# The last six first-layer weight units of an attention and maxout kernel: an integer add and a subtraction in place of identity products on TensorE, and new ranks in the planner

## The chip, the cores and the metric

The kernel runs on one core of one Trainium2 chip. The metric is the device time of one execution, in microseconds (us). The engines are TensorE (PE in the rows; its weight loads are PEld), VectorE (DVE), ScalarE (ACT), GpSimd (POOL) and SyncE (SP), which issues most DMAs.

## The reference

Attention over 8 batches, 8 heads, 576 positions and 64 values a head, with a mask that lets a position see its own block of 64 and all blocks before it; its output, 4608 tokens of 512 values, goes through three products of which the largest is kept, and through a last product:

```python
scores = np.matmul(q, k.transpose(0, 1, 3, 2)) / np.sqrt(D)
scores = np.where(mask, scores, -1000000000.0)     # mask: block_i >= block_j, blocks of 64
attn = np.exp(scores - np.max(scores, axis=-1, keepdims=True))
attn = attn / (np.sum(attn, axis=-1, keepdims=True) + 1e-09)
attn_out = np.matmul(attn, v)
x = attn_out.transpose(0, 2, 1, 3).reshape(B * S, H * D)
h = np.maximum(np.maximum(x @ w1, x @ w2), x @ w3)  # 512 -> 768
out = h @ w_out                                     # 768 -> 512
```

The weights reach the chip as 64-bit numbers, and each is read as a low and a high 32-bit word; q, k and v have 32 bits.

## The kernel before

**Pairs.** Attention goes by pairs of heads: 8 batches of 4 pairs, numbered 0 to 31. For each pair TensorE makes the scores (L924, L931), VectorE the row maxima (L448), ScalarE the exponentials (L615, L950), ScalarE and GpSimd the normalised values (L464, L466). From batch 1 on VectorE turns them (L635, L639) into the tile pz, SyncE moves pz to pt by DMA (L645), and TensorE multiplies pt by v (L1005); batch 0 is turned on TensorE (L569, L976). VectorE also turns q and k (L908).

**Chunks.** The second half of the program goes by nine chunks of 512 tokens. Chunks 0 to 7 are the first 512 positions of batches 0 to 7; chunk 8 gathers the remaining 64 positions of all batches. A chunk needs the x of its four pairs, each split into a rounded part xh (ScalarE) and a rest xl (a subtraction, L261, on GpSimd or VectorE). Then 18 products, one for each weight unit of the first layer (216 matmuls, L1129), with the largest of three kept in the tile m (L1142); then the projection through w_out (72 matmuls, L1163), whose left side is m split into hh and hl. There is one m: the products of the next chunk beyond its first one wait for the projection.

**Weight units.** A weight unit is a tile of 128 by 512 weights. Units 0 to 17 belong to the first layer (w1, w2, w3 in turn for each of six column blocks), units 18 to 23 to w_out. A unit is loaded by SyncE (L308) and rebuilt from its words into a rounded part h and a rest l. For units 0 to 17 the steps are: `size` (ScalarE, L331), `clamp` (L336), `shift` (L343), `sign` (L349), `power` (L360), `rest` (L370), all five on VectorE; `high` (ScalarE, a cast at L256); `summed`, three matmuls with an identity or its negative (L376 to L378) that add up the value, minus h, plus the rest in PSUM; and `lower_summed`, a cast from PSUM (ScalarE, L256). Units 18 to 23 have `size`, `tail` (L326, ScalarE or VectorE), `clamp`, `shift`, `sign`, `whole` (an int32 add, L357), `high`, and `lower`, the subtraction of h from the value (L261, GpSimd or VectorE). Temporaries lie in the tiles wo0 to wo3 for units 0 to 17, with wo4 or wo5 as a spare until the sum is made; the w_out units use wo4, wo5 and the two osb tiles, and are themselves kept in wo0 to wo5. The negative identity lies in one of the osb tiles.

**The order.** No engine's order is written out. Each step is a job with a rank, a modelled duration for each engine that may do it, the jobs that it follows and the buffers that it takes. `in_order` plays the jobs on the modelled engines: whenever an engine is idle, it takes the ready job of lowest rank. The order that comes out is what each engine then does. Ranks come from a few numbers: pair p of batch 0 has rank p x FIRST_PAIR, later pairs follow in steps of PAIR, unit u has DELAY + PACE x u (its load 8 less), and a chunk spreads its products over the ranks from its start to the next chunk's start, where a start is the rank behind its batch's last pair, plus END.

Of the kernel before, what the change touches and what calls it, by code (L numbers as in the profile page):

```python
# [143 lines left out]
def pe(*cols, least=128):  # L144
    return sum(max(n, least) / 2.4 + 13.5 for n in cols)


def dve(n, fast=False):
    return 68.0 + n / (1.92 if fast else 0.96)


def act(n, psum=True):
    return (52.0 if psum else 88.0) + n / 1.2


def pool(n):
    return 150.0 + 2.15 * n
# [3 lines left out]
def kernel(  # L161
# [19 lines left out]
    NF = DF // P  # L181
    NT = 4
    HALF = (256, 320)
    SCALE = 0.125
    DELAY = 28.0
    PACE = 3.5

    PAIR = 24
    FIRST_PAIR = 14
    TURN = 12  # L190

    SECOND = 9
    NEAR = 4
    END = 40
    N = 512

    slots = dict(
# [48 lines left out]
    def job(cost, rank, call, *args, after=(), take=(), give=(), lasts=0.0, moved=0.0, ports=False):  # L246
        j = Job(cost, rank, lambda eng: call(eng, *args), after, take, give, lasts, moved, ports)
        jobs.append(j)
        return j
# [14 lines left out]
    class Unit:  # L264


        def __init__(self, u, src, dst, n, prior, *early, first=None):
            self.src, self.dst, self.n, self.u = src, dst, n, u
            self.last = n == DO
            rank = DELAY + PACE * u  # L270


            self.tag = f"wo{dst}" if self.last else f"w{u}"
            self.temps = (f"wo{u % 4}",) if not self.last else (f"wo{4 + dst % 2}",) if dst < 4 else ("osb", "osb")
            j = self.issued = job(
                {"SP": SEND},
                rank - 8,
                self.load,
                after=(prior and prior.issued, first, *(e.sized for e in early if e)),
                take=(self.tag,) if self.last else (),  # L280
            )
            j = job({}, 0, lambda eng: None, after=(j,), lasts=MOVE, moved=1600.0)
            j = self.sized = job({"ACT": act(512, False) + 65.0}, rank, self.size, after=(j,), take=self.temps)
            if not self.last:
                spare = f"wo{4 + u % 2}"
                for step, fast in (
                    (self.clamp, True),
                    (self.shift, True),
                    (self.sign, False),
                    (self.power, True),  # L290
                    (self.rest, False),
                ):
                    c = dve(512, fast) + (5.0 if fast else 5.0)
                    j = job({"DVE": c}, rank, step, after=(j,), take=(spare,) if step == self.rest else (), lasts=c + GAP, ports=True)
                j = job({"ACT": act(512, False)}, rank, self.high, after=(j,))
                j = job({"PE": 6 * pe(512)}, rank, self.summed, after=(j,), take=("pm",), give=(*self.temps, spare))
                self.done = job({"ACT": act(512)}, rank, self.lower_summed, after=(j,), give=("pm",))
                return
            k = job({"ACT": act(512, False) + 65.0, "DVE": dve(512) + 5.0}, rank, self.tail, after=(j,))
            for step, fast in ((self.clamp, True), (self.shift, True), (self.sign, False), (self.whole, False)):  # L300
                c = dve(512, fast) + (5.0 if fast else 5.0)
                j = job({"DVE": c}, rank, step, after=(j, k) if step == self.whole else (j,), lasts=c + GAP, ports=True)
            h = job({"ACT": act(512, False)}, rank, self.high, after=(j,))
            self.done = job({"POOL": pool(512), "DVE": dve(512) + 5.0}, rank, self.lower, after=(h,), give=self.temps, ports=True)
# [90 lines left out]
    units, begun = {}, []  # L395

    def weights():
        u, prior, early = 0, None, []
        for f in range(NF):
            for i, w in enumerate((w1, w2, w3)):  # L400
                prior = units[i, f] = Unit(
                    u, w[:, f * P : (f + 1) * P].rearrange("(c p) f -> p c f", p=P), (i, f), P, prior, early[u - NEAR] if u >= NEAR else None, first=begun[min(u + 1, NP - 1)]
                )
                early.append(prior)
                u += 1
        for f in range(NF):
            prior = units["out", f] = Unit(
                u,
                w_out[f * P : (f + 1) * P, :].rearrange("(c p) f -> p c f", p=P),
                f,  # L410
                DO,
                prior,
                early[2 * NF + f],
                early[u - 2],
            )
            early.append(prior)
            u += 1
# [41 lines left out]
    def norm_cost(n):  # L459
        return {"POOL": 250.0 + 1.5 * n, "ACT": 190.0 + n / 1.2}  # L460
# [7 lines left out]
    class Head:  # L468
# [5 lines left out]
        def plan(self, t0):  # L474

            pair, part, self.exps, self.inv = self.pair, self.pair.part, {}, {}
            for n, ts in enumerate(part.groups):
                apart, r = None, t0 + (SECOND if part.beside and ts == part.later else n)
                for t in ts:
                    m = P * (t + 1)  # L480
                    d = job(
                        {"DVE": dve(m) + 20.0},
                        r + 1,
                        self.top,
                        t,
                        after=(pair.scored[ts], apart, pair.began),
                        take=("stat",) if pair.began is None else (),
                    )
                    pair.began = pair.began or d
                    if t != ts[-1]:  # L490
                        apart = job({}, 0, lambda eng: None, after=(d,), lasts=GAP)
                    self.exps[t] = job({"ACT": act(m) + 200.0}, r + 2, self.exp, t, after=(d,), take=(f"p{t}",))
                join([self.exps[t] for t in ts], BANK)

        def turns(self, t0, after):
# [4 lines left out]
            for t in part.tiles:  # L500
                r = t0 + 8 + t / 2 + (SECOND if part.beside and t in part.later else 0)
                self.scales[t] = job(norm_cost(P * (t + 1)), r, self.scale, t, after=(self.inv[t],))
# [146 lines left out]
    class Pair:  # L649
# [11 lines left out]
        def plan(self, first, before):  # L661
# [42 lines left out]
            if part.beside:  # L704
                self.later = job(
                    {"PE": cost[part.later] + 200.0 + before.cost},
                    first + SECOND,
                    self.both,
# [3 lines left out]
                self.scored[part.later] = self.later  # L712
                before.finish(self.later, first + SECOND)
            else:
# [8 lines left out]
            for j, h in enumerate(self.heads):  # L723
                h.plan(first + 4 * j)
            for r, ts in ((first + 7, [t for g in part.first for t in g]), (first + SECOND + 5, part.later)):
                r = r if ts != part.later or part.beside else first + 8
# [455 lines left out]
    made = []  # L1182

    def plan(b, part, gap):
        nonlocal rank
        pairs = [Pair(b, hp, part, len(made) + hp) for hp in range(NP)]
        for p in pairs:
            p.plan(rank, made[-1] if made else None)
            made.append(p)
            rank += gap  # L1190
        return pairs

    rank = 0
    pairs, starts = [], []
    for b in range(B):
        pairs.append(plan(b, PLAIN if b == 0 else EARLY if b == 1 else WHOLE, PAIR if b else FIRST_PAIR))
        starts.append(rank + END)
    made[-1].alone(rank + SECOND)
    starts += [starts[-1] + NP * PAIR, starts[-1] + 2 * NP * PAIR]
    weights()  # L1200
    last = units[2, NF - 1].done
    job({"SP": 1.0}, -100, lambda eng: None, take=("osb",))
    join((last,), ("osb",))

# [36 lines left out]
```

## Time and profile before

| what | value |
|---|---|
| median of 3 runs | 894.97 us (894.92 to 895.81) |
| time of the profiled execution | 897.37 us |
| its span, first to last instruction | 895.6 us |
| TensorE busy | 873.8 us, 98% |
| VectorE busy | 561.5 us, 63% |
| ScalarE busy | 443.3 us, 50% |
| GpSimd busy | 148.7 us, 17% |
| granted TensorE clock | 1.000 over the whole span |

The shares are means over stages that differ. The records of matmuls overlap, since they are pipelined, so 98% does not say that every matmul follows the one before at full pace; the start of one to the start of the next does.

### The profile page before, as it was taken

What the parts mean: (1) busy time and instruction counts of PE and PEld (TensorE: products, weight loads), DVE (VectorE), ACT (ScalarE), POOL (GpSimd) and SP (SyncE); (2) the same over time, 40 slices, a digit from 0 to 9 for tenths busy, and PEclk for the clock granted to TensorE, in tenths of its full rate; (3) what the DMA queues carried; (4) which work ended last, traced back from release to release, by engine and by line L of the source; (5) the groups of instructions that cost most, each with busy time, mean ns of one, the idle gap of its engine ahead of it and who ended that gap; (6) DMA issues with size and microseconds to landing.
All of it is one profiled execution on the core that took longest, in us unless ns stands there. A gap on an engine that the chain in (4) does not pass through costs nothing.

```text
span 895.6 us, 13551 instructions
## 1 busy us (share of the span) xinstructions
PE 873.8 (98%) x4436; PEld 647.3 (72%) x4436; DVE 561.5 (63%) x1545; ACT 443.3 (50%) x1225; POOL 148.7 (17%) x179
## 2 busy tenths in 40 slices
PE   6889999999999999999999999999999999999997
PEld 4666667767777767777767777777777778888886
DVE  4799999968767576837773876477656732122121
ACT  5677577666546354645555454555455523013012
POOL 1001214321113012301221121212130201001000
PEclk9999999999999999999999999999999999999999
DMA  6565546676665266526654565555555430000002
GB/s 151 166 175 135 118 103 192 131 162 140 136 138 125 66 134 138 120 89 132 126 119 117 119 127 118 127 125 115 114 137 112 112 74 36 12 0 36 12 1 47
DMA packets 228549, 97.10 MB, mean 108 GB/s; under 512 B 185216, under 2 KB 223104, under 8 KB 228480
## 3 DMA queue, kind: packets, MB, share of 16 engines
q1 hardware_dynamic: 214208, 93.89, 45.3%
q10 hardware_dynamic: 14272, 2.36, 1.5%
q8 instruction: 35, 0.57, 0.3%
q14 instruction: 34, 0.28, 0.1%
HBM read 40.89 MB, written 9.44 MB: 56 GB/s over the span
## 4 chain that ended last, share of the span: by engine, by line
PE 86%; DVE 7%; ACT 2%; DMA 1%; SPq 1%; issue 1%; DVEq 0%; ACTq 0%
PE pm L1129 47%; PE pm L1163 16%; PE sb L1005 9%; PE sb L924 8%; PE sb L931 3%; DVE sb L448 2%; PE sb L569 2%; PE pm L376 1%; DVE pz L635 1%; SPq L645 1%; DMA pt<-pz 1%; ACT p L615 1%; DVE kq L908 0%; DVE m L1142 0%; ACT p L950 0%
## 5 line engine op out<-in xcount | busy, mean ns | idle before, releaser
L1129 PE MATMUL pm<-xh,w 128*128 128x512 f32 x1296 | 434.0, 403 | 0.0
L1129 PEld LDWEIGHTS pm<-xh,w 128*128 128x128 f32 x1296 | 243.3, 188 | 64.9 <-issue 13.2
L1129 PE MATMUL pm<-xl,w 128*128 128x512 f32 x648 | 253.2, 391 | 0.8 <-POOL xl L261 0.8
L615 ACT ACTIVATE p<-sb,nm 128x512 f32<-128x512 f32 (+3 forms) x256 | 133.6, 527 | 89.7 <-DVE nm L448 88.3
L448 DVE CUSTOM_DVE_ANT_0 sb<-sb,mask 128x512 f32<-128x512 f32 (+3 forms) x288 | 143.3, 528 | 53.8 <-PE sb L931 36.4
L635 DVE STREAM_TRANSPOSE pz<-p 128x512 f32<-128x512 f32 (+1 forms) x280 | 138.1, 528 | 38.8 <-ACT p L464 24.4
L466 POOL TENSOR_TENSOR p<-p,rs 128x128 f32<-128x128 f32 (+3 forms) x107 | 73.4, 704 | 464.7 <-DVE rs L759 407.9
L1142 DVE TENSOR_TENSOR m<-pm,m 128x512 f32<-128x512 f32 x108 | 73.2, 678 | 110.7 <-PE pm L1129 108.7
L1129 PEld LDWEIGHTS pm<-xl,w 128*128 128x128 f32 x648 | 121.9, 188 | 28.1 <-issue 4.5
L1163 PE MATMUL pm<-wo,hh 128*128 128x512 f32 x432 | 133.4, 390 | 0.4 <-ACT hh L256 0.4
L1163 PEld LDWEIGHTS pm<-wo,hh 128*128 128x128 f32 x432 | 80.9, 188 | 17.9 <-ACT hh L256 1.0
L1005 PE MATMUL sb<-pt,vn 128*64 128x320 f32 (+2 forms) x840 | 91.7, 361 | 1.4 <-DMA pt<-pz 1.3
L924 PE MATMUL sb<-kq 64*128 64x128 f32 (+3 forms) x512 | 88.5, 463 | 2.9 <-DVE rs L759 1.4
L1005 PEld LDWEIGHTS sb<-pt,vn 128*64 128x64 f32 x840 | 56.1, 137 | 40.3 <-issue 10.6
L1163 PE MATMUL pm<-wo,hl 128*128 128x512 f32 x216 | 84.2, 390 | 0.6 <-DVE hl L261 0.6
L924 PEld LDWEIGHTS sb<-kq 64*128 64x128 f32 x512 | 45.3, 189 | 44.7 <-issue 20.8
L256 ACT COPY m<-pm 128x512 f32<-128x512 f32 x54 | 31.5, 583 | 87.7 <-PE pm L1129 87.6
L464 ACT ACTIVATE p<-p,rs 128x384 f32<-128x384 f32 (+3 forms) x117 | 64.3, 591 | 20.7 <-DVE rs L759 20.6
L261 DVE TENSOR_TENSOR hl<-m,hh 128x384 fp32r<-128x384 f32 x55 | 34.0, 627 | 52.5 <-ACT hh L256 51.8
L256 ACT CAST hh<-m 128x384 fp32r<-128x384 f32 x72 | 35.1, 512 | 56.3 <-PE pm L1163 40.9
L256 ACT COPY x<-sb 128x256 f32<-128x256 f32 x59 | 22.0, 374 | 59.6 <-PE sb L1005 59.4
L615 ACT ACTIVATION_READ_ACCUMULATOR p<-sb,nm 128x1 f32 x256 | 50.9, 199 | 0.0
(91 smaller groups left out, 742.1 us busy)
## 6 DMA issues: line engine op xcount, KB each, us to landing
pt<-pz SPq DMA_DIRECT2D x224, 200.0 KB, 3.9
w<-in_moe_w_dram SPq DMA_DIRECT2D x18, 512.0 KB, 5.3
vn<-in_v_dram SPq DMA_DIRECT2D x64, 128.0 KB, 2.3
out_dram<-osb SPq DMA_DIRECT2D x32, 256.0 KB, 2.0
nat<-in_k_dram SPq DMA_DIRECT2D x112, 72.0 KB, 2.3
nat<-in_q_dram SPq DMA_DIRECT2D x96, 72.0 KB, 2.4
wo<-in_moe_w_out_dram SPq DMA_DIRECT2D x6, 512.0 KB, 4.1
nat<-in_q_dram ACTq DMA_DIRECT2D x16, 72.0 KB, 3.4
```

The lines of the kernel that those rows point to most:

```text
L256: nc.scalar.copy(dst, src)
L261: {"DVE": nc.vector, "POOL": nc.gpsimd}[eng].tensor_tensor(out=dst, in0=a, in1=b, op=ALU.subtract)
L448: nc.vector.tensor_tensor_reduce(out=ps, in0=ps, in1=hidden, scale=-SCALE, scalar=first, op0=ALU.add, op1=ALU.min, accum_out=out_)
L464: nc.scalar.mul(p, p, r)
L466: nc.gpsimd.tensor_tensor(out=p, in0=p, in1=r.broadcast_to([P, p.shape[1]]), op=ALU.mult)
L615: nc.scalar.activation(dst, src, AF.Exp, bias=nm[:, c : c + 1], scale=-1.0, accum_out=sm[:, c : c + 1])
L635: nc.vector.transpose(dst, p[:, 0 : n * P])
L924: nc.tensor.matmul(ps, self.q[h.own, P * t : P * (t + 1)], self.k[h.own, 0:w], start=True, stop=True)
L1005: nc.tensor.matmul(o[h.own].rearrange("p (i u) -> p i u", u=n)[:, :, c0 : c0 + z - a], self.vn[:, kt, h.j, :], h.pt[:, :, a:z], start=(m = ...
L1129: nc.tensor.matmul(self.ps, w[i, f][:, c, :], xx, start=(c == 0 and s == 0), stop=(c == NC - 1 and s == 2))
L1142: nc.vector.tensor_tensor(out=m, in0=ps, in1=m, op=ALU.max)
L1163: nc.tensor.matmul(self.po, h, w[f], start=(f == 0 and s == 0), stop=(f == NF - 1 and s == 2))
```

## The change

Units 12 to 17 go the way of the w_out units: `tail` and `whole` in place of `power` and `rest`, and `lower` in place of `summed` and `lower_summed`. They no longer take a PSUM bank or the spare tile. The negative identity's osb tile is given back after unit 11 and not after unit 17. The constants of the planner's ranks are changed, and units, the first twelve pairs and the chunks get corrections of their own.

```diff
-    DELAY = 28.0
+    DELAY = 28.1
     PACE = 3.5
-    PAIR = 24
-    FIRST_PAIR = 14
+    PAIR = 24.0
+    FIRST_PAIR = 12.7
     TURN = 12
     SECOND = 9
+    SUMMED = 12
+    UNITS = (0, 0, 0, 0, -1, 0, 0, 4, 9, 9, 1, 9, 9, 9, 9, 8, 8, 8, 8, 8, 8, 8, 8, 7)
+    PAIRS = (0, 0, 0, 0, 0, 0, 0, 0, -2, -2, -4, -2)
+    STARTS = (-1, -1, -2, -1, -1, -1, -1, -1, 3, -1, 2)
     NEAR = 4
-    END = 40
+    END = 33.6
...
-            rank = DELAY + PACE * u
+            rank = DELAY + PACE * u + UNITS[u]
...
-            if not self.last:
+            if u < SUMMED:
                 spare = f"wo{4 + u % 2}"
...
-            p.plan(rank, made[-1] if made else None)
+            p.plan(rank + (PAIRS[len(made)] if len(made) < len(PAIRS) else 0), made[-1] if made else None)
...
     starts += [starts[-1] + NP * PAIR, starts[-1] + 2 * NP * PAIR]
+    starts = [a + d for a, d in zip(starts, STARTS)]
     weights()
-    last = units[2, NF - 1].done
+    last = [x for x in units.values() if x.u < SUMMED][-1].done
```

The steps that units 12 to 17 now take are those of the w_out units:

```python
def tail(self, eng):    # b = low_word * 2**-29, as int32; ACT or DVE
def whole(self, eng):   # a = a + b, int32; DVE
def lower(self, eng):   # l = a - h; POOL or DVE
```

## Rows read from the trace of the kernel before

**Rows 1.** The page: busy time, share of the span and instructions of each engine.
```profile
PE 873.8 (98%) x4436; PEld 647.3 (72%) x4436; DVE 561.5 (63%) x1545; ACT 443.3 (50%) x1225; POOL 148.7 (17%) x179
```

**Rows 2.** Busy time by stretch: PE, PEld, DVE, ACT, POOL, then PE's clock and DMA.
```profile
45.00:95.00 50.00, 45.36 (x284) 30.81 (x281) 48.97 (x147) 38.65 (x110) 9.67 (x10) 1.00 0.58 146
95.00:130.00 35.00, 34.71 (x153) 22.32 (x153) 34.21 (x86) 21.39 (x53) 4.84 (x5) 1.00 0.44 100
130.00:178.80 48.80, 48.80 (x252) 35.34 (x249) 47.38 (x125) 33.98 (x89) 18.38 (x18) 1.00 0.70 169
...
203.90:762.00 558.10, 556.72 (x2847) 410.24 (x2846) 359.47 (x1009) 285.79 (x815) 99.81 (x121) 1.00 0.52 115
```

**Rows 3.** Chain that ended last, 86 to 128 us: start, length, what.
```profile
93.25 1.38 DVE wo L360
...
108.55 0.86 PE pm L376 x2
109.41 0.23 PE pm L377
109.64 0.24 PE pm L378
...
119.74 0.59 ACT w L256
...
127.55 0.86 PE pm L376 x2
```

**Rows 4.** The same chain where TensorE is full: 204 products in a row.
```profile
762.51 46.24 PE pm L1129 x204
```

**Rows 5.** Unit steps, 95 to 130 us: count, duration ns min/median/max, first and last start.
```profile
L370 DVE SCALAR_TENSOR_TENSOR wo<-w,wo x8: 679/684/691, 94.7 to 126.1; 128x512 fp32r<-128x512 uint32 x8
...
L360 DVE TENSOR_SCALAR wo<-wo x7: 389/423/427, 97.7 to 125.0; 128x512 int32<-128x512 int32 x7
```

**Rows 6.** The w_out units' own steps: the tail, the integer add, the subtraction.
```profile
L326 ACT ACTIVATE wo<-wo x4: 654/670/692, 131.9 to 145.2; 128x512 int32<-128x512 uint32 x4
...
L357 DVE CUSTOM_DVE_ANT_0 osb<-osb x2: 643/666/689, 158.1 to 164.7; 128x1024 uint16<-128x1024 uint16 x2
...
L261 POOL TENSOR_TENSOR wo<-osb,wo 128x512 fp32r<-128x512 f32 x2 | 2.6, 1296 | 8.4 <-ACT p L615 5.8 <-ACT wo L256 2.6
```

**Rows 7.** The cast from PSUM, 85 to 130 us, on ScalarE: count, busy us, mean ns.
```profile
L256 ACT CAST w<-pm 128x512 fp32r<-128x512 f32 x9 | 5.2, 578 | 2.4 <-PE pm L378 2.4
```

**Rows 8.** VectorE and GpSimd around the w_out subtractions: start, duration, instruction.
```profile
143.39 1.49 DVE L343 TENSOR_SCALAR wo<-wo 128x512 int32<-128x512 int32 x1
...
146.94 0.41 DVE L343 TENSOR_SCALAR wo<-wo 128x512 int32<-128x512 int32 x1
...
148.41 1.44 DVE L357 CUSTOM_DVE_ANT_0 wo<-wo 128x1024 uint16<-128x1024 uint16 x1
...
143.30 1.29 POOL L261 TENSOR_TENSOR wo<-wo,wo 128x512 fp32r<-128x512 f32 x1 [1.33 <-ACT wo L256]
```

**Rows 9.** L1129 alone by stretch: PE busy (matmuls), PEld busy (loads).
```profile
95.00:150.80 55.80, 31.86 (x133) 24.30 (x132) 1.00 0.55 138
```

**Rows 10.** From chunk 0 to chunk 1: GpSimd and TensorE by time.
```profile
166.63 1.30 POOL L261 TENSOR_TENSOR wo<-osb,wo 128x512 fp32r<-128x512 f32 x1 [5.79 <-ACT p L615]
...
192.24 1.30 POOL L261 TENSOR_TENSOR xl<-x,xh 128x512 fp32r<-128x512 f32 x1 [5.31 <-ACT xh L256]
...
182.78 0.62 PE L1163 MATMUL pm<-wo,hh 128*128 128x512 f32 x2
...
186.30 2.93 PE L1005 MATMUL sb<-pt,vn 128*64 128x320 f32 x28
...
202.14 0.50 PE L1129 MATMUL pm<-xh,w 128*128 128x512 f32 x1
```

**Rows 11.** Loads of units, SyncE's queue: count, issue ns, first and last issue.
```profile
L308 SPq DMA_DIRECT2D w<-in_moe_w_dram x18: 367/510/977, 9.5 to 93.0; - x18
L308 SPq DMA_DIRECT2D wo<-in_moe_w_out_dram x6: 340/349/1167, 123.7 to 151.9; - x6
```

## The prediction

> **What bounds the kernel now.** I read the page first, then the stretches, then the chain of waits in the stretch where the changed units run, and last the order of events between chunk 0 and chunk 1. The page says that TensorE is busy nearly the whole span and VectorE 63% [rows 1]; the reader should not stop at that, since both are means. From 203.9 us on TensorE is busy 556.72 of 558.10 us and VectorE 359.47 [rows 2]: there TensorE alone sets the time, and whatever reaches that point earlier ends earlier by as much. Before it there are two full engines. From 45 to 95 us VectorE is busy 48.97 of 50 and TensorE 45.36; from 95 to 130 VectorE 34.21 of 35 and TensorE 34.71; from 130 to 178.8 VectorE 47.38 of 48.8 and TensorE all of it [rows 2]. A full engine is a bound only if somebody waits for it. Between 108 and 128 us the chain runs through TensorE, and the identity products stand in it [rows 3]; TensorE's work there is not cover for something else, it is the path. VectorE is full in the same stretch because it works ahead: it finishes weights long before they are used (below).
>
> **What leaves TensorE.** The chain has one unit's sum as 0.86 + 0.23 + 0.24 = 1.33 us (L376 to L378), back to back [rows 3]. Six such sums, those of units 12 to 17, stand in it from 108.55 to 127.55. 6 x 1.33 = 7.98 us of a full TensorE go. The price is no artefact of overlapping records: 204 products in a row take 46.24 us, 0.227 each [rows 4], and a sum costs as much as six of them, 1.36. No other TensorE instruction is added.
>
> **What leaves and comes on the other engines.** VectorE loses `power`, 0.423, and `rest`, 0.684 [rows 5], and gets `whole`, 0.666 [rows 6]: 0.44 less a unit, 2.6 for six. ScalarE loses the cast from PSUM, 0.578 [rows 7], and gets the tail, 0.670 [rows 6]: 0.09 more, 0.6 for six, covered because ScalarE is busy 21.39 of 35 [rows 2]. The tails of the w_out units stand on ScalarE; were the new ones on VectorE, the nearest row is the 0.666 of the add, which would turn the 2.6 saved into 1.4 more. GpSimd gets `lower`, 1.30 a unit [rows 6], 7.8 in all, where it is busy 4.84 of 35 and 18.38 of 48.8 [rows 2]. One cast from PSUM stands in the chain, 0.59 at 119.74, ahead of exponentials that TensorE then waits for [rows 3]; without it I count 0.6 more gained.
>
> **What GpSimd does to VectorE.** During the subtraction that starts at 143.30 and takes 1.29, VectorE's `shift` takes 1.49, against 0.41 for the same step at 146.94 [rows 8]: 1.08 lost. An integer add at 148.41 takes 1.44 against 0.666, 0.77 lost. Those are the two large ones beside six subtractions. The bounds for six new ones are 0 (only transposes or maxima run beside them) and 6 x 1.08 = 6.5; I take what the six old ones lost, 1.08 + 0.77 = 1.85. VectorE then ends 2.6 - 1.85 = 0.8 less loaded, which I count as nothing.
> The Trainium skill, SBUF — State Buffer, "SBUF: two separate sides", speaks against the change here: VectorE and GpSimd share a pair of ports that one instruction holds exclusively until it ends, if VectorE runs a two-port mode or reads two SBUF tensors. The row at 143.39 agrees. Taken to its end, each of six subtractions would hold VectorE for its whole 1.29 us, 7.7, and VectorE would be 7.7 - 2.6 = 5.1 later; that is a rival below.
>
> **What is moved.** Ranks are priorities, not times, but near one us each: 24 of them take one pair. Pair 3 goes from rank 42 to 38.1, pair 4 from 56 to 50.8, and all pairs behind by 5.2, pairs 8 to 11 by 2 to 4 more. Units 8 and 9 go from 56 and 59.5 to 65.1 and 68.6, unit 12 from 70 to 79.1, the last w_out unit from 108.5 to 115.6. Chunk 0 starts at 83.4 instead of 96, chunk 1 at 179.4 instead of 192. So attention goes ahead of weights, and products ahead of both.
> Are the six units late then? 133 of the 144 products of units 0 to 11 run between 95.0 and 150.8 [rows 9], so unit 12's first product falls near 150.8, while its sum was made at 108.55 and that of unit 17 by 129. Even 10 us later they keep over 20 us; the move costs nothing, covered by the products of eleven units. Their loads move with them by 9 ranks; the eighteen are issued by 93.0, a stretch ahead of use [rows 11]. The w_out loads stand on SyncE behind the six units, whose tiles they take: 123.7 for the first [rows 11] becomes some 132 with 8.1 ranks more. If SyncE waits there, the q and k loads and the pz moves of the next pairs wait behind it. The earlier return of the osb tile is worth nothing: the integer adds of the units that take it come at 158.1 [rows 6], long after either return.
> The w_out units have less room. The last subtraction ends at 166.63 + 1.30 = 167.9, and the projection reads column block 5 first at 182.78 [rows 10]. With TensorE 8.6 earlier that is 174.2, and the unit, 8.1 later by rank, comes at 176.0: 1.8 us short. Pair 7's product with v, 2.93, can stand in that gap [rows 10], as can two blocks of three products of chunk 1, 1.4. I count nothing, and keep 1.8 for the range.
> The next limit is pair 7. Its x is complete at 192.24 + 1.30 = 193.5, and chunk 1 needs it behind the three products at 202.14, at 202.8 [rows 10]. TensorE 8.6 earlier reads it at 194.2. It fits, with 0.7 to spare, if VectorE is no later.
> The value of the other rank moves: at best they recover TensorE's idle time from 45 to 95, 50 - 45.36 = 4.6, for VectorE's unit steps do stand in the chain there, 1.38 at 93.25 [rows 2, 3]; at worst they add a wait. I take nothing.
>
> **The sum.** 8.0 + 0.6 = 8.6 us. The profiled execution took 897.37 us, of which 895.6 is span; it would take 888.8. Against the median of the runs, 894.97, which is 2.4 lower, that is 886.4.
>
> **The rivals.** *The start tightens too.* Units 8 to 11 leave VectorE to pairs 3 and 4, chunk 0 starts earlier, and the 4.6 us idle go: 881.8. For it speaks the chain at 93.25; against it pair 7's x, which lets TensorE gain only 0.7 more unless VectorE, full from 45 on, brings pair 7 earlier as well.
> *VectorE gives some back.* With every subtraction costing 1.08 on VectorE, it is 6.5 - 2.6 = 3.9 later, pair 7's x comes at 197.4, and TensorE, wanting it at 194.2, waits 3.2: 889.6. For it speaks that VectorE has no idle time up to 178.8; against it that four of six old subtractions cost little. By the skill's port rule alone, taken to its end, x comes at 198.6 and the time is 890.8. If SyncE's wait on the w_out tiles holds the moves of pz as well, nothing may be left of the gain: 894 to 896.
> *The w_out units are late: slower.* One mechanism: they are 8 ranks later on a full VectorE, behind pairs that were pulled forward, and the projection waits for the last of them, while m is not free for chunk 1. It costs more than the change gives once the last subtraction ends past 174.2 + 8.6 = 182.8, 14.9 later than now, and is measurably slower past 184.6. A slip of 20 us gives 900. For it: only the rank order protects them. Against: the slip by rank is 8.1.
> *The change doesn't shorten the path*, because TensorE runs dry elsewhere by the same 8 us: this is the 894 to 896 above.
>
> **How the numbers follow.** The likeliest: the sums go and little else, 884 to 889.5, chance 0.48. Tightened start, 878 to 884: 0.20. Some given back, 889.5 to 893.2: 0.16. Nothing left, within 0.2% (1.8 us, about what a measurement of this kernel can tell): 0.07. Slower than 896.8: 0.09. So faster 0.84, same 0.07, slower 0.09. The range of 8 in 10 leaves out the last two and the lowest fifth of the tightened start: 880 to 893.
>
> **What would show it.** L376 to L378 with 12 sums and not 18; six more subtractions into w on GpSimd at some 1.3 us, six more integer adds; fast VectorE steps of over 1 us beside them. TensorE enters its even stretch some 8 to 9 us earlier than 203.9, with x of pair 7 near 193 and no new idle time between 165 and 200. The prediction is wrong if TensorE shows waits for pair 7's x, for w_out units or for pt there, or if 45 to 95 us loses or gains more than 2 us of TensorE idle time.

## The result and the profile after

The changed kernel takes 887.04 us (median of 5 runs, 886.79 to 887.76), the kernel before 895.54 beside it (894.92 to 895.81): 8.5 us less, ratio 0.9907, 95% interval 0.9893 to 0.9922. The forecast was 886.4. The number was right; two of the steps under it were not, and the experiments are about those.

The page of after, as in [rows 1]:

```profile
PE 864.2 (98%) x4412; PEld 641.9 (73%) x4412; DVE 559.5 (63%) x1534; ACT 443.9 (50%) x1215; POOL 156.6 (18%) x200
```

Busy time by stretch in after, columns as in [rows 2]:

```profile
45.00:95.00 50.00, 45.45 (x284) 31.07 (x281) 47.93 (x149) 37.84 (x111) 8.20 (x10) 1.00 0.52 128
95.00:130.00 35.00, 35.00 (x166) 25.64 (x165) 33.49 (x85) 23.86 (x59) 7.47 (x8) 1.00 0.73 170
130.00:178.80 48.80, 46.81 (x236) 33.55 (x235) 48.46 (x121) 36.07 (x94) 22.33 (x20) 1.00 0.60 149
195.30:762.00 566.70, 566.58 (x2900) 417.82 (x2899) 363.42 (x1015) 288.25 (x806) 104.28 (x138) 1.00 0.52 115
```

The stretch from 195.3 begins 8.6 before the 203.9 of [rows 2], but it is not the same point of the work. One point can be found in both traces: from 203.86 us before and from 196.37 after, the same 3412 matmuls are left to TensorE, line by line. Up to that point and from it on, first before, then after:

```profile
0.00:203.86 203.86, 188.24 (x1025) 131.19 (x1026) 175.23 (x498) 135.95 (x370) 43.26 (x53) 1.00 0.61 149
203.86:895.60 691.74, 685.52 (x3412) 516.06 (x3410) 386.25 (x1048) 307.39 (x855) 105.43 (x126) 1.00 0.43 96
...
0.00:196.37 196.37, 180.77 (x1002) 128.11 (x1003) 171.81 (x487) 135.22 (x371) 46.65 (x57) 1.00 0.61 151
196.37:884.70 688.33, 683.42 (x3412) 513.77 (x3410) 387.70 (x1049) 308.64 (x844) 109.90 (x143) 1.00 0.44 98
```

The changed kernel is there 7.5 us earlier. TensorE was busy 7.5 less (180.77 for 188.24) and stood still as long as before (15.60, 15.62). From 45 to 95 it is as busy as before, so the start did not tighten. From 95 to 130 it has no gap and does 166 matmuls where it did 153; from 130 to 178.8 it now stands still for 2.0. The spans of the two traces differ by 10.9 us. The other 3.4 lie behind that point: TensorE waits 1.3 less there (in the even stretch 0.12, before 1.38 [rows 2]) and takes 2.1 less for the same matmuls. The medians differ by 8.5; the profiled execution of before (897.37) lay 1.8 above its median, so the traces show more gain than the medians do.

The unit steps in after, count, duration min/median/max in ns, first and last start; the forms as in [rows 5, 6]:

```profile
L380 PE MATMUL pm<-wo,plus x24: 591/592/697, 36.5 to 105.1; 128*128 128x512 f32 x24
L361 DVE CUSTOM_DVE_ANT_0 wo<-wo x10: 655/682/1485, 107.4 to 154.5; 128x1024 uint16<-128x1024 uint16 x10
L265 POOL TENSOR_TENSOR w<-wo,w x5: 1276/1296/1478, 109.7 to 135.0; 128x512 fp32r<-128x512 f32 x5
L265 DVE TENSOR_TENSOR w<-wo,w x1: 692/692/692, 125.7 to 125.7; 128x512 fp32r<-128x512 f32 x1
```

Twelve sums are left (two products of the kind shown in each). Of the six new subtractions the order puts five on GpSimd and one on VectorE. Around them, in after's timeline (start, duration, instruction; in brackets the idle time before it and what ended it), then more of the same view up to chunk 1:

```profile
109.72 1.48 POOL L265 TENSOR_TENSOR w<-wo,w 128x512 fp32r<-128x512 f32 x1
110.68 0.54 DVE L759 TENSOR_SCALAR rs<-sm 128x6 f32<-128x6 f32 x1
...
118.66 1.36 DVE L912 STREAM_TRANSPOSE kq<-nat 128x1152 f32<-128x1152 f32 x1
...
129.68 1.28 POOL L265 TENSOR_TENSOR w<-wo,w 128x512 fp32r<-128x512 f32 x1 [9.69 <-ACT w L260]
130.36 1.16 DVE L353 SCALAR_TENSOR_TENSOR wo<-w,wo 128x512 int32<-128x512 int32 x1
...
140.89 1.30 POOL L265 TENSOR_TENSOR wo<-wo,wo 128x512 fp32r<-128x512 f32 x1 [4.63 <-ACT wo L260]
141.09 1.13 DVE L759 TENSOR_SCALAR rs<-sm 128x6 f32<-128x6 f32 x1
...
173.04 0.50 PE L1167 MATMUL pm<-wo,hh 128*128 128x512 f32 x1 [0.63 <-DVE wo L265]
...
189.67 1.30 POOL L265 TENSOR_TENSOR xl<-x,xh 128x512 fp32r<-128x512 f32 x1 [2.89 <-ACT xh L260]
```

And the chain that ended last in after (start, length, what). From 108 to 118 us, where [rows 3] had TensorE, it now runs through VectorE, and from there to 173 through VectorE again with steps of ScalarE and GpSimd and transfers between; TensorE takes it over only then:

```profile
107.53 0.55 DVE wo L361
...
113.09 1.13 DVE wo L361
...
168.86 1.43 DVE osb L361
...
172.20 0.80 DVE wo L265
173.04 6.88 PE pm L1167 x29
```

### The profile page after: what moved, and what is told of

The parts are those of the page before. It is cut to its first block, busy times and chain, and to the rows that moved or that the text cites. A ratio compares the mean times of both kernels' runs of the same rounds, so it can differ in the third digit from the quotient of the medians.

```text
span 884.7 us, 13483 instructions
## 1 busy us (share of the span) xinstructions
PE 864.2 (98%) x4412; PEld 641.9 (73%) x4412; DVE 559.5 (63%) x1534; ACT 443.9 (50%) x1215; POOL 156.6 (18%) x200
## 4 chain that ended last, share of the span: by engine, by line
PE 83%; DVE 9%; ACT 3%; DMA 2%; issue 1%; POOL 0%; SPq 0%; ACTq 0%; DVEq 0%; POOLq 0%
PE pm L1133 46%; PE pm L1167 16%; PE sb L1009 9%; PE sb L928 7%; PE sb L935 3%; DVE sb L452 2%; PE sb L573 1%; ACT p L619 1%; DMA wo<-in_moe_w_out_dram 1%; DVE wo L340 1%; DVE pz L639 1%; DVE wo L353 1%; DVE kq L912 1%; DMA pt<-pz 0%; DVE rs L759 0%
## 5 line engine op out<-in xcount | busy, mean ns | idle before, releaser
L1133 PEld LDWEIGHTS pm<-xh,w 128*128 128x128 f32 x1296 | 243.4, 188 | 63.0 <-issue 10.5
L619 ACT ACTIVATE p<-sb,nm 128x128 f32<-128x128 f32 (+3 forms) x256 | 133.6, 528 | 61.7 <-DVE nm L452 60.1
L639 DVE STREAM_TRANSPOSE pz<-p 128x512 f32<-128x512 f32 (+1 forms) x280 | 136.3, 524 | 20.8 <-ACT p L468 14.1
L470 POOL TENSOR_TENSOR p<-p,rs 128x128 f32<-128x128 f32 (+3 forms) x124 | 78.8, 659 | 393.2 <-DVE rs L763 307.5
L1167 PEld LDWEIGHTS pm<-wo,hh 128*128 128x128 f32 x432 | 80.2, 188 | 20.5 <-ACT x L260 1.7
L265 DVE TENSOR_TENSOR hl<-m,hh 128x384 fp32r<-128x384 f32 x58 | 40.8, 703 | 42.9 <-ACT hh L260 42.6
L468 ACT ACTIVATE p<-p,rs 128x512 f32<-128x512 f32 (+3 forms) x100 | 58.7, 612 | 14.6 <-DVE rs L763 14.0
L265 POOL TENSOR_TENSOR xl<-x,xh 128x512 fp32r<-128x512 f32 x30 | 40.0, 1348 | 43.2 <-ACT xh L260 42.7
```

The lines of the kernel that those rows point to most:

```text
L265: {"DVE": nc.vector, "POOL": nc.gpsimd}[eng].tensor_tensor(out=dst, in0=a, in1=b, op=ALU.subtract)
L468: nc.scalar.mul(p, p, r)
L470: nc.gpsimd.tensor_tensor(out=p, in0=p, in1=r.broadcast_to([P, p.shape[1]]), op=ALU.mult)
L619: nc.scalar.activation(dst, src, AF.Exp, bias=nm[:, c : c + 1], scale=-1.0, accum_out=sm[:, c : c + 1])
L639: nc.vector.transpose(dst, p[:, 0 : n * P])
L1133: nc.tensor.matmul(self.ps, w[i, f][:, c, :], xx, start=(c == 0 and s == 0), stop=(c == NC - 1 and s == 2))
```

## The experiments

The theory from the forecast: TensorE's sums are the path, the rank moves are worth nothing. The rivals: the removed sums alone gain nothing, and the ranks carry the gain; or GpSimd's subtractions take part of it back. All medians in us; each stands beside runs of the kernel before on the same chip, and "change" is the difference of these two medians.

| run | median | before beside it | change | ratio, 95% interval |
|---|---|---|---|---|
| the change itself | 887.04 | 895.54 | -8.5 | 0.9907 [0.9893, 0.9922] |
| e1_units_only | 901.33 | 895.62 | +5.7 | 1.0051 [1.0038, 1.0064] |
| e2_ranks_only | 896.42 | 895.62 | +0.8 | 1.0005 [0.9996, 1.0015] |
| e3_pe_time_back | 893.30 | 895.62 | -2.3 | 0.9970 [0.9959, 0.9981] |
| e4_subtract_twice | 889.99 | 895.62 | -5.6 | 0.9941 [0.9929, 0.9953] |
| e5_unit_ranks_old | 893.93 | 895.96 | -2.0 | 0.9978 [0.9968, 0.9988] |
| e6_pair_chunk_ranks_old | 895.54 | 895.96 | -0.4 | 0.9993 [0.9983, 1.0004] |
| e7_six_summed | 897.34 | 895.96 | +1.4 | 1.0010 [0.9999, 1.0020] |
| e8_subtract_on_vector | 887.88 | 895.96 | -8.1 | 0.9908 [0.9894, 0.9922] |
| e9_units_only_pe_back | 908.47 | 896.09 | +12.4 | 1.0137 [1.0120, 1.0154] |
| e10_ranks_a_little_off | 888.54 | 896.09 | -7.6 | 0.9916 [0.9902, 0.9931] |
| e11_out_units_earlier | 886.94 | 896.09 | -9.2 | 0.9899 [0.9885, 0.9914] |
| e12_order_before_kept | 898.32 | 895.80 | +2.5 | 1.0032 [1.0020, 1.0045] |

**The two halves: e1 and e2.** e1 is the kernel before with the six units by integer add and subtraction, every rank as it was:

```diff
+    SUMMED = 12
-            if not self.last:
+            if u < SUMMED:
-    last = units[2, NF - 1].done
+    last = [x for x in units.values() if x.u < SUMMED][-1].done
```

> The kernel before with units 12 to 17 on the integer add and the subtraction, and every rank as before. If TensorE's 8.0 us of sums are the gain and the moved ranks are worth nothing, as the prediction counted, it takes about 887 us, 8 to 9 under the kernel before. If VectorE, which the trace after shows on the chain up to 173 us, lets TensorE keep the gain only because pairs were moved ahead of units, the units alone give less: 890 to 894. If the ranks alone are the gain, it stays at 895.

e2 is the changed kernel with all eighteen units summed on TensorE again, the new ranks kept:

```diff
-    SUMMED = 12
+    SUMMED = 18
```

> The changed kernel with all eighteen first-layer units summed on TensorE again, and the new ranks. By the prediction's sum it takes 895, within 1.5 us of the kernel before. If the ranks bring what the units alone do not, it takes 889 to 893. If the new ranks only fit the shorter TensorE work and hurt without it, 897 or more.

The units alone make the kernel 5.7 us slower (4.6 by the ratio of all executions), the ranks alone move it by less than its interval, both together take 8.5 off. So neither half has a value of its own: with the old ranks the new units cost 5.7, with the new ranks they save 9.3 (-8.5 against +0.8). That the sums come off the path whatever the ranks is refuted. In e1 TensorE waits where it had none; busy time by stretch in e1 (profiled execution 903.06), columns as above:

```profile
150.00:160.00 10.00, 6.88 (x38) 4.27 (x39) 9.03 (x30) 7.25 (x23) 3.59 (x4) 0.85 0.41 124
160.00:230.00 70.00, 62.92 (x319) 44.43 (x319) 54.34 (x154) 40.71 (x117) 22.13 (x25) 1.00 0.60 131
```

And from e1's timeline VectorE's turn of q and k for pair 6:

```profile
135.02 1.33 DVE L909 STREAM_TRANSPOSE kq<-nat 128x1152 f32<-128x1152 f32 x1
```

The same stretches in before:

```profile
150.00:160.00 10.00, 10.00 (x48) 7.48 (x47) 9.98 (x30) 8.43 (x21) 4.22 (x6) 1.00 0.67 164
160.00:230.00 70.00, 69.24 (x353) 49.08 (x353) 54.26 (x164) 44.13 (x130) 18.78 (x20) 1.00 0.67 148
```

The same turn in before:

```profile
127.41 1.35 DVE L908 STREAM_TRANSPOSE kq<-nat 128x1152 f32<-128x1152 f32 x1
```

The turn, without which pair 6 has no scores, comes at 127.41 in before, 135.02 in e1 and 118.66 in after.

**Which ranks: e5, e6, e10.** e5 is the changed kernel with the old ranks of the units, e6 with the old ranks of pairs and chunks:

```diff
-    DELAY = 28.1
-    UNITS = (0, 0, 0, 0, -1, 0, 0, 4, 9, 9, 1, 9, 9, 9, 9, 8, 8, 8, 8, 8, 8, 8, 8, 7)
+    DELAY = 28.0
+    UNITS = (0,) * 24
```

> The changed kernel with the old ranks of the units (no corrections by unit, DELAY 28.0); pairs and chunks keep their new ones. The units alone had cost 901.3 and the whole change 887.0, so 14 us hang on the ranks. If it is the units' delay that frees VectorE for the pairs, this is near 901, 897 or more. If it is the earlier pairs and chunks, it stays within 2 us of 887. If any set of ranks gives its own order and time, without a rule, it lies in between.

```diff
-    FIRST_PAIR = 12.7
-    PAIRS = (0, 0, 0, 0, 0, 0, 0, 0, -2, -2, -4, -2)
-    STARTS = (-1, -1, -2, -1, -1, -1, -1, -1, 3, -1, 2)
-    END = 33.6
+    FIRST_PAIR = 14
+    PAIRS = ()
+    STARTS = (0,) * 11
+    END = 40
```

> The changed kernel with the old ranks of pairs and chunks (FIRST_PAIR 14, END 40, no corrections); the units keep their new delays. The counterpart of the run before it: if the units' delay is what matters, 885 to 890; if the earlier pairs and chunks are, 897 or more.

Counted from e1, the ranks of pairs and chunks are worth 5.7 + 2.0 = 7.7 and those of the units 5.7 + 0.4 = 6.1; together 14.2, nearly the sum. Both do the same thing to the turn of pair 6: it comes at 127.3 in e5, at 126.1 in e6. Of the four kernels that differ in ranks alone the one with the latest turn is the slowest and the one with the earliest the fastest: turn at 135.0, 127.3, 126.1, 118.7; change +5.7, -2.0, -0.4, -8.5. The two between stand the other way round, and with all sums left a turn at 127.41 (before) or 114.0 (e2) comes with no gain. So the turn goes along with the time; that it alone decides it is not shown. VectorE's work on units ahead of that turn (busy time for tile wo alone; the third is VectorE's), in before:

```profile
0.00:127.40 127.40, 24.46 (x52) 8.92 (x53) 49.80 (x90) 22.37 (x36) 0.00 (x0) 1.00 0.56 141
```

And in after:

```profile
0.00:118.70 118.70, 16.81 (x36) 6.27 (x36) 39.33 (x72) 24.07 (x39) 2.87 (x3) 1.00 0.58 147
```

Ahead of the turn stand 72 unit steps for 90, 10.5 us less: the twelve steps of three units now come behind it, and six steps have left VectorE altogether. The turn comes 8.75 earlier.

e10 sets the ranks between the two:

```diff
-    FIRST_PAIR = 12.7
+    FIRST_PAIR = 13.1
-    END = 33.6
+    END = 34.4
```

> The changed kernel with FIRST_PAIR 13.1 instead of 12.7 and END 34.4 instead of 33.6, a small step back towards the old values. If the ranks work by a rule (pairs ahead of units) the time moves by under 2 us: 886 to 889. If the order that the planner happens to find decides, it jumps: 890 or more.

About 1 us of the gain goes (-7.6 against -8.5, intervals overlapping; the turn at 120.3). At this neighbouring setting the gain holds, so it does not hang on one exact order.

**Is it the removal, or a worse order in e1? e12.** The planner orders every engine anew as soon as a unit's steps change, so e1 changes the order too. e12 plans the kernel before as it was and keeps each engine's order; only what units 12 to 17 issue in their slots is exchanged:

```diff
         def size(self, eng):
...
+            if 12 <= self.u < 18:
+                self.tail("ACT")
         def power(self, eng):
+            if 12 <= self.u < 18:
+                return
         def rest(self, eng):
+            if 12 <= self.u < 18:
+                return self.whole(eng)
         def summed(self, eng):
+            if 12 <= self.u < 18:
+                return self.lower("POOL")
         def lower_summed(self, eng):
+            if 12 <= self.u < 18:
+                return
```

> The kernel before, planned as it was, so that every engine keeps its order; only the steps of units 12 to 17 are swapped where they stand: the tail right behind size on ScalarE, the integer add in place of the rest, the subtraction on GpSimd where the three matmuls stood, and power, the matmuls and the cast from PSUM left away. The units alone, planned anew with the old ranks, took 901.3. If those 6 us are the new order that the planner found, and not the steps, this one keeps TensorE's gain: 887 to 890. If GpSimd's hold of VectorE or VectorE's own work eats the gain whatever the order, it stays at 893 to 897 or is slower.

It is slower by 2.5 us. So the exchange gains nothing in the old order, and the first outcome written down, that the planner's order alone was to blame, did not come; that order accounts at most for the remaining 3.2 of e1, and since the intervals of e1 and e12 overlap, not surely for that. Where did 8 us of TensorE go? Busy time by stretch in e12, first the whole, then the part at half the granted clock (0.50):

```profile
108.00:130.00 22.00, 16.31 (x66) 10.32 (x64) 21.42 (x52) 14.21 (x36) 9.61 (x9) 0.84 0.30 76
...
121.30:128.10 6.80, 6.07 (x15) 3.97 (x14) 6.22 (x21) 4.62 (x16) 3.42 (x4) 0.50 0.41 121
```

Before, the same stretch:

```profile
108.00:130.00 22.00, 21.87 (x99) 13.47 (x99) 21.32 (x60) 15.42 (x39) 3.61 (x4) 1.00 0.33 83
```

TensorE does 66 matmuls for 99, of which 24 were the sums, and stands still, while VectorE is as full as before with 52 instructions for 60. What TensorE waits for, and the two engines at one subtraction, in e12's timeline:

```profile
113.63 2.24 PE L1015 MATMUL sb<-pt,vn 128*64 128x320 f32 x18 [1.62 <-DMA pt<-pz]
117.82 0.70 PE L934 MATMUL sb<-kq 64*128 64x256 f32 x2 [1.32 <-ACT p L625]
119.46 0.87 PE L1015 MATMUL sb<-pt,vn 128*64 128x256 f32 x8 [0.95 <-ACT p L625]
...
118.35 1.27 POOL L261 TENSOR_TENSOR w<-wo,w 128x512 fp32r<-128x512 f32 x1 [3.27 <-ACT w L256]
118.46 1.70 DVE L351 SCALAR_TENSOR_TENSOR wo<-w,wo 128x512 int32<-128x512 int32 x1
...
128.69 1.35 DVE L918 STREAM_TRANSPOSE kq<-nat 128x1152 f32<-128x1152 f32 x1
```

It waits for exponentials and their turned copies, whose inputs VectorE prepares between its unit steps. And VectorE's unit steps from 108 to 130 us, in e12 (x5, busy us, mean ns):

```profile
L338 DVE TENSOR_SCALAR wo<-wo 128x512 f32<-128x512 f32 x5 | 4.4, 896 | 0.0
L351 DVE SCALAR_TENSOR_TENSOR wo<-w,wo 128x512 int32<-128x512 int32 x5 | 4.3, 878 | 0.0
L359 DVE CUSTOM_DVE_ANT_0 wo<-wo 128x1024 uint16<-128x1024 uint16 x5 | 3.3, 678 | 0.0
L345 DVE TENSOR_SCALAR wo<-wo 128x512 int32<-128x512 int32 x5 | 2.5, 509 | 0.0
```

The same groups in before, and the two that leave:

```profile
L336 DVE TENSOR_SCALAR wo<-wo 128x512 f32<-128x512 f32 x5 | 2.0, 413 | 0.0
L349 DVE SCALAR_TENSOR_TENSOR wo<-w,wo 128x512 int32<-128x512 int32 x5 | 3.3, 681 | 0.0
L343 DVE TENSOR_SCALAR wo<-wo 128x512 int32<-128x512 int32 x5 | 2.0, 421 | 0.0
L360 DVE TENSOR_SCALAR wo<-wo 128x512 int32<-128x512 int32 x5 | 2.0, 421 | 0.0
L370 DVE SCALAR_TENSOR_TENSOR wo<-w,wo 128x512 fp32r<-128x512 uint32 x5 | 3.3, 687 | 0.0
```

VectorE loses 2.0 + 3.3, gets 3.3, and pays (4.4 - 2.0) + (4.3 - 3.3) + (2.5 - 2.0) = 3.9 beside the subtractions: 1.9 more. The turn of pair 6 comes at 128.69, 1.3 later than before. The chain that ended last in e12 runs through VectorE up to that turn, with the stretched steps in it, where before has TensorE [rows 3]:

```profile
107.55 1.63 DVE wo L338 x2
...
118.59 1.57 DVE wo L351
...
128.77 1.28 DVE kq L918
```

VectorE, not TensorE, sets the pace of this order, and without their sums TensorE's products only wait. How much of this is the subtractions' hold on VectorE and how much its own work is not separated: e12 takes the sums out and puts the subtractions in, and the sums were not taken out by themselves.

The point with 3412 matmuls left, the same ones in each trace, shows what became of the time saved in every order with twelve sums (us; "at half clock" is the time up to that point with a granted clock near 0.50):

| kernel | point reached | TensorE busy before it | standing still | at half clock |
|---|---|---|---|---|
| before | 203.86 | 188.24 | 15.62 | 0 |
| after | 196.37 | 180.77 | 15.60 | 0 |
| e10 | 199.29 | 184.13 | 15.16 | 6.8 |
| e5 | 203.76 | 184.68 | 19.08 | 6.8 |
| e6 | 205.30 | 185.16 | 20.14 | 10.2 |
| e12 | 205.25 | 183.44 | 21.81 | 6.8 |
| e1 | 207.89 | 183.25 | 24.64 | 3.4 |

All but before have the same matmuls up to there. Of the 7.5 that after saves, e12 loses 6.2 by standing still and 2.7 by half clock. What e5 and e6 lose against after is about half standing still and half the clock, and both of e5's stretches at half clock (15.3 to 18.7, 76.8 to 80.2) lie ahead of the turn of pair 6. So the ranks' effect is not the turn of pair 6 alone. The clock is not all of it either: one of e12's twelve executions had a mean granted clock of 1.000 and took 898.08, near their median. The profiled execution of e12 took 896.5 and its median is 898.32, so its loss in the median is larger than this point shows.

**Is TensorE the path in the changed kernel? e3 and e9.** e3 adds 36 products in chunk 0, 8.2 us by their price in [rows 4], to the changed kernel (they issue wl times xh a second time for units 3 to 11):

```diff
+                if s == 0 and self.b == 0 and 3 <= 3 * f + i < 12:
+                    nc.tensor.matmul(self.ps, wl[i, f][:, c, :], xh, start=False, stop=False)
```

> The changed kernel in its own order, with 36 matmuls of 512 columns more in chunk 0 (the product of the weights' rest with xh is made twice in units 3 to 11, so the output counts that small term twice there). At 0.227 us each they give TensorE 8.2 us back, as much as the six sums took, and leave every other engine as it is. If TensorE's time is the path in that stretch, it takes 894.5 to 895.5 (8.2, less the 0.6 us that TensorE waits for the last w_out unit at 173 us). If VectorE sets the pace and TensorE merely follows, 887 to 890.

6.2 of the 8.2 come back. Part of the rest fell into the waits that after has: from 95 to 178.8 it is busy 35.00 + 46.81 = 81.81 of 83.80, 2.0 short, and in e3 nothing is short:

```profile
95.00:178.80 83.80, 83.80 (x413) 60.82 (x411) 76.27 (x188) 56.65 (x144) 25.38 (x24) 1.00 0.60 147
```

Up to the point with 3412 matmuls left, 203.20 in e3, TensorE is busy 188.84 and stands still 14.36: 8.1 more and 1.2 less than in after. With the new ranks time added to TensorE lengthens the kernel but for that little. e9 makes the same addition to e1:

```diff
+    SUMMED = 12
+                if s == 0 and self.b == 0 and 3 <= 3 * f + i < 12:
+                    nc.tensor.matmul(self.ps, wl[i, f][:, c, :], xh, start=False, stop=False)
```

> The kernel of the units alone (old ranks, 901.3) in its own order, with the 36 extra matmuls of the run e3, 8.2 us of TensorE, in chunk 0, units 3 to 11. In its trace TensorE stands still some 13 us longer before 230 us than in the kernel before. If that is because VectorE's chain of pairs is late and TensorE runs out of products, most of the 8.2 us fall into the waits: 901 to 904. If TensorE's work is on the path there too, 907 to 909.5.

If TensorE merely ran out of products in e1, the addition was to fall into its waits. It costs 6.7 (12.4 - 5.7), so this fell: the turn of pair 6 moves from 135.0 to 141.1, and up to the same point (215.21) TensorE still stands still 23.37. The two engines follow each other in a fixed order, and what delays TensorE's scores delays VectorE's next step; this is argued, no run parts it. Idle time of TensorE is therefore no cover in itself. And e3 does not tell the two kernels apart: added time is paid in both. That TensorE is the path in after and not in e1 rests on what it stands still there, 15.60 and 24.64, and on the sums' removal, which gains only with the new ranks.

**What GpSimd's subtractions cost: e4 and e8.** Both keep the order of after. e4 issues each of the six subtractions twice:

```diff
-            minus(eng, self.l, self.a, self.h.bitcast(F32))
+            for _ in range(1 if self.last else 2):
+                minus(eng, self.l, self.a, self.h.bitcast(F32))
```

> The changed kernel in its own order, with the subtraction of units 12 to 17 issued twice in a row on its engine (five on GpSimd, one on VectorE). If GpSimd's subtractions cost nothing that anyone waits for, as the prediction counted, it stays within 1 us of the changed kernel, 886.5 to 888. If each holds VectorE by up to 1.08 us and VectorE's chain to the last w_out unit is tight, TensorE waits 2 to 6 us longer near 173 us: 889 to 893.

e8 issues the six on VectorE:

```diff
-            minus(eng, self.l, self.a, self.h.bitcast(F32))
+            minus(eng if self.last else "DVE", self.l, self.a, self.h.bitcast(F32))
```

> The changed kernel in its own order, with the subtractions of units 12 to 17 all on VectorE (five move there from GpSimd at the place in the order that they have). Each takes 0.69 on VectorE, 3.5 us in all, and takes away what GpSimd's five held VectorE for, 1.8 by the trace after. If VectorE is tight, the net 1.7 us show: 888 to 889.5. If it is not, 887.

The second six cost 2.9 (-5.6 against -8.5); on VectorE, where five more of them take 5 x 0.692 = 3.5, the time is that of after within the intervals (-8.1). Where they run makes no difference that these runs can tell; doubling them does, in part through the clock: in e4's trace it is 0.50 for 3.4 us from 140.9.

**How far it goes: e7 and e11.** e7 takes six more units off TensorE, ranks as in after:

```diff
-    SUMMED = 12
+    SUMMED = 6
```

> The changed kernel with units 6 to 11 on the integer add as well, so that six sums are left on TensorE. They stood at 72 to 106 us, where TensorE has waits of its own. If only what lies in TensorE's full stretch counts, the two or three sums from 95 us on go: 2.7 to 4 us, 883 to 884.5. If VectorE sets the pace there, more subtractions on GpSimd hold it and nothing is gained or something lost: 887 to 895.

All of the gain goes, +1.4. Busy time in e7 from 150 to 180 us, and a part of it:

```profile
150.00:180.00 30.00, 20.01 (x63) 10.56 (x62) 28.65 (x66) 18.50 (x49) 12.93 (x12) 0.67 0.49 110
...
153.70:167.30 13.60, 9.76 (x24) 4.95 (x24) 13.51 (x24) 5.43 (x12) 6.76 (x5) 0.50 0.41 99
```

VectorE is busy 28.65 of 30 us, TensorE does 63 matmuls in them, much of the time at half clock. That fits VectorE setting the pace again with more sums gone, but it was not tried apart from the clock, and the ranks were those chosen for twelve sums.

e11 gives the w_out units ranks 2 to 3 lower, against the wait of 0.63 at 173.04:

```diff
-    UNITS = (0, 0, 0, 0, -1, 0, 0, 4, 9, 9, 1, 9, 9, 9, 9, 8, 8, 8, 8, 8, 8, 8, 8, 7)
+    UNITS = (0, 0, 0, 0, -1, 0, 0, 4, 9, 9, 1, 9, 9, 9, 9, 8, 8, 8, 5, 5, 5, 5, 5, 5)
```

> The changed kernel with the six w_out units 3 ranks earlier (2 the last). The trace after shows TensorE waiting 0.63 us at 173 us for the last of them. If that wait is the only thing that their rank decides, 886.4 to 887. If VectorE is so tight that what comes earlier pushes the pairs back, 888 to 893.

The same as after, within the intervals. No version here beats the changed kernel measurably.

## Why the prediction was right, and where its steps were not

- *The even stretch sets the time, and reaching it earlier is the gain.* Right in kind: the same work is left 7.5 earlier, forecast 8 to 9. In the traces 3.4 more come behind that point, where the forecast had nothing.
- *Six sums of 1.33 leave TensorE.* Right in size: twelve sums are left, TensorE is busy 7.5 less up to the same point, forecast 8.0, and its time given back in e3 costs 6.2 of 8.2.
- *"TensorE's work there is not cover for something else, it is the path."* This step failed for the kernel before. The chain showed the sums, back to back [rows 3], but two engines were full there, and a chain shows one of two nearly equal ways. With the sums out and the order kept (e12), TensorE stands still 6.2 longer up to the same point and the kernel is 2.5 slower. The sentence that VectorE "is full because it works ahead" was half of the truth: some of the units that it worked ahead on stood in front of pair 6.
- *The rank moves: "I take nothing".* This step failed too, and hid the first failure. Without them the change costs 5.7; with them it saves 8.5. I had looked for their worth in TensorE's idle time from 45 to 95 alone, 4.6, which did not change (45.45 busy, 45.36 before). Their worth was that TensorE stands still no longer than before once the sums are out: 15.60 up to the same point, where the old ranks, wholly or in part, leave 19.08 to 24.64, and 3.4 to 10.2 us at half clock besides. The steps of three units go behind the turn of pair 6; that this is how the ranks do it is argued.
- So the sum came out right by two errors of opposite sign: removal alone, forecast -8.6, measured +2.5 to +5.7; ranks, forecast 0, measured -11.0 to -14.2 on top of it. Counted the other way round both terms come out as forecast: the ranks first, +0.8 for 0, then the removal, -9.3 for -8.6. The prediction gave no reason for that order and said that the sums were the path in the kernel before, so its number was in part luck.
- *GpSimd costs VectorE 1.85.* Too much for after: beside the five I find 0.54 for some 0.16 at 110.68 and 1.16 for 0.69 at 130.36, 0.85 in all (the integer add of 1.485 stands beside another subtraction of GpSimd, that of hl). Too little for the old order: 3.9 for five (e12). Both lie inside the bounds of 0 and 6.5; what stands beside a subtraction is the order's doing. The Trainium skill, SBUF — State Buffer, "SBUF: two separate sides", has one of the two engines hold the shared ports until its instruction ends. The traces agree in kind: even an operation on 128x6 takes 1.13 at 141.09, beside the subtraction at 140.89. They do not show VectorE held for the whole of each subtraction: 3.9 for five is 0.78 us of the 1.29 of each, and 0.85 for five is 0.17. That section of the Trainium skill limits the hold to VectorE instructions in a two-port mode or with two SBUF inputs, so this is no disagreement; which of the instructions here are such no run shows. The expectation of e8 put the hold in after at 1.8; by the steps counted here it is 0.85.
- *The cast of 0.6 in the chain.* Not tried by itself; it stays a term without a measurement. The 7.5 up to the same point leave no room for it.
- *The last w_out unit, 1.8 short at 176.0.* By the prediction's own ranks, 108.5 to 115.6, this unit slips by 7.1 and not by 8.1, which makes it 0.8 short. It ends at 172.99, and TensorE waits 0.63 for it. A wait for w_out units was named as a sign of being wrong, so by that sign this step was; the kernel before waits as long, 0.64, for hl at 181.73. e11 shows nothing measurable in it: its trace still has the wait, 0.64.
- *Pair 7's x near 193.5, in time.* It is complete at 190.97, and TensorE waits for it nowhere.
- The rivals: the start did not tighten. Of "VectorE gives some back" the mechanism was real in the old order (e12, e1), and the new ranks took it out of the path. *The w_out units are late* did not come.

Open: whether the planner's order in e1 costs more than e12 at all (3.2 by the medians, 4.6 and 2.9 by the ratios, with intervals that overlap), and why the new ranks with all sums left (e2) gain nothing though pair 6's turn comes at 114.0 there. From 130 to 178.8 us TensorE is busy 46.12 and VectorE 44.87 of 48.8 in e2, so neither is full there, and what holds it was not tried.

## What to carry to other kernels

Where two engines are full, the chain of waits names one of them; before counting work that leaves it as gain, take that work out in the unchanged order (as e12) and see whether the time falls. If it does not, the other engine's order has to change with it: put what it prepares long ahead behind what the first engine waits for next. And such a shift has an end: six more units moved the same way, at the same ranks, gave all of it back (e7).

## What was not expected of the hardware

TensorE's granted clock fell to half, 1.2 of 2.4 GHz, for 6.8 us from 121.30 in e12, after it had stood still for 1.62, 1.32 and 0.95 us within seven us, and for 13.6 us in e7; before and after show 1.00 in every stretch read. A short wait in a dense stretch can so cost more than itself. e10 comes nearest to a price: with the same matmuls up to the same point as after, and no more standing still (15.16, 15.60), TensorE is busy 3.4 us longer (184.13, 180.77), with 6.8 us at a granted clock of 0.50. And a subtraction on GpSimd stretched VectorE's small 128x6 operation as much as a 128x512 one: 1.13 at 141.09, against 0.16 for the same step at 67.93.
